# Power-of-two scales computed for pairs of attention units, all queue orders made anew, and more warming matmuls in the opening

## The chip, the cores and the metric

The kernel runs on one core of a Trainium2 chip. The time is device microseconds of one execution. PE is TensorE, DVE VectorE, ACT ScalarE, POOL GpSimd, SP the SyncE queue that issues all the kernel's transfers.

## What is computed

Attention with random features, then a feed-forward layer on all tokens. From the reference, cut:

```python
# q, k, v: 8 batches x 8 heads x 576 x 64; omega: 128 x 64
q_s, k_s = q / 64 ** .25, k / 64 ** .25
phi(x): h = x @ omega.T - sum(x * x) / 2;  exp(h - max(h)) / sqrt(128)
kv, z = phi(k_s).T @ v, sum over tokens of phi(k_s)
attn  = (phi(q_s) @ kv) / (phi(q_s) @ z + 1e-6)
x     = attn as 4608 tokens x 512
h     = x @ w_in                      # 512 x 2048
out   = max(0.01 * h, h) @ w_out      # 2048 x 512
```

## The kernel before

**Tiling.** The 4608 tokens are nine blocks of 512 (0 to 8). Heads go in pairs (`hp` 0 to 3). A *unit* is one pair of heads in one batch of keys or one block of queries: its features are 4 or 5 tiles of 128 tokens x 2 heads x 128 features. A key batch ends in the sums `kv` (L1262 in the opening, L1274 to L1276 later); a query block multiplies its features by them (L1388, L1381), divides (`r`, L1401 and L1403; `xp`, L1405) and turns the result into the input `xt` of the feed-forward layer (L1328 and L1331 in the opening, a DMA transpose L1316 later).

**The opening.** Key batches 0 and 1 and query block 0 are units of class `Whole`: inputs come transposed (L1106, tiles `nat`, `t`, `xn`, by their places in memory), PE multiplies in fp32 (L1133, 16 matmuls into the bank `pj`; the fifth tile of a key unit goes to `pj0` and `edge`), DVE takes the maximum (L1149) and subtracts it (L1151, into `ph`), ACT takes the exponent. At the same time the weights `w_in` and `w_out` are loaded in 1 MB pieces (L877), rebuilt from their halves of words (L892 to L922) and split into two fp16 parts (L758, L963).

**The omega constants.** `omega()` loads omega (L820) and the 128 x 128 identity (`ident`, L821). DVE scales omega and takes its largest magnitude (L832, L833), PE spreads that over all partitions by a product with `ident` (L799), DVE makes a power of two of it (L804 to L809) and `split` makes the fp16 `om` and the factor `om_c` (L838 to L843). The power and `split` are needed by units of class `Unit` only, thus not by the opening's fp32 units.

**The later units, class `Unit`.** There are 56: 24 key units (key batches 2 to 7, four pairs of heads each) and 32 query units (query blocks 1 to 8). `prepare()` loads `nat` (L1000), ACT squares it into `z` and adds the squares of each partition into column 0 of `sc` (L1003), DVE sums the squares of each head (`sq`, L1005) and makes four factors on 128 x 1 (L1010, L1012, L1014, L1015). They scale the halves of fp16 written into `z`, which a DMA transpose turns into `t` (L1028). PE then projects (L1041), and the features follow as above.

**The feed-forward layer.** Blocks 0 and 1 use plain products in the first layer (L1541), blocks 2 to 8 products with fewer multiplications whose weights come from memory through a ring (L1595); the second layer is L1777, in the last two blocks L1702. Sums go to the banks `ffn` and `late`.

**The order of the work.** It is written out: `ORDER` lists all operations by number, `ON` names the engine of those that have a choice, `PLACES` the buffer that each tile gets. Each engine executes its part of `ORDER` in that order, so an operation that waits holds all behind it on its engine. A negative number in `ORDER`, −n, is n warming matmuls on PE: a product of `ident` with itself (L850, 128 x 240) that nobody reads. They lie in a part of a bank that `mi` also has, so some wait for that bank.

Of the kernel before, what the change touches and what calls it, by code (L numbers as in the profile page):

```python
# [17 lines left out]
P = 128  # L18
# [63 lines left out]
    "raw": [0, 1, 3, 2, 0, 1, 3, 2, 3, 0, 1, 2],  # L82
    "sqz": [0, 1, 2, 0, 1, 2, 0, 1, 2, 0, 1, 2],
# [1800 lines left out]
```

## Time and profile before

| | |
|---|---|
| time, median of 3 runs (lowest to highest) | 902.92 us (900.46 to 908.13) |
| time of the profiled execution, and its span | 904.01 us, 902.2 us |
| mean granted clock of TensorE | 0.994 |
| PE, PEld (weight loads, which overlap PE) | 97%, 70% |
| DVE, ACT, POOL | 82%, 62%, 37% |

An engine's share is its busy time over the span. The granted clock is in parts of 2.4 GHz. A line such as L1149 is a line of the kernel before; where the kernel after is quoted, its own lines are used, with the old line beside them.

### The profile page before, as it was taken

What the parts mean: (1) busy time and instruction counts of PE and PEld (TensorE: products, weight loads), DVE (VectorE), ACT (ScalarE), POOL (GpSimd) and SP (SyncE); (2) the same over time, 40 slices, a digit from 0 to 9 for tenths busy, and PEclk for the clock granted to TensorE, in tenths of its full rate; (3) what the DMA queues carried; (4) which work ended last, traced back from release to release, by engine and by line L of the source; (5) the groups of instructions that cost most, each with busy time, mean ns of one, the idle gap of its engine ahead of it and who ended that gap; (6) DMA issues with size and microseconds to landing.
All of it is one profiled execution on the core that took longest, in us unless ns stands there. A gap on an engine that the chain in (4) does not pass through costs nothing.

```text
span 902.2 us, 20554 instructions
## 1 busy us (share of the span) xinstructions
PE 879.3 (97%) x8136; PEld 632.3 (70%) x8136; DVE 740.9 (82%) x1438; ACT 556.0 (62%) x997; POOL 330.6 (37%) x387
## 2 busy tenths in 40 slices
PE   6899999999999999999999999999999999999998
PEld 5786645555557865687558765876588656888887
DVE  6999999898988889878877998888878768884662
ACT  5789897678746775568647864763565633632430
POOL 1332557465343435225331622333222421331341
PEclk9999999999999999999999999999999999999999
...
GB/s 365 269 179 202 148 156 174 200 245 106 171 250 258 237 217 156 220 250 207 224 203 236 223 185 230 199 203 168 175 206 253 172 96 179 140 111 153 129 1 48
DMA packets 274881, 170.13 MB, mean 189 GB/s; under 512 B 191072, under 2 KB 237920, under 8 KB 273760
## 3 DMA queue, kind: packets, MB, share of 16 engines
...
q8 instruction: 63, 1.03, 0.5%
q14 instruction: 34, 0.28, 0.1%
HBM read 105.87 MB, written 16.78 MB: 136 GB/s over the span
## 4 chain that ended last, share of the span: by engine, by line
PE 80%; DVE 9%; DMA 5%; ACT 3%; issue 1%; SPq 1%; POOL 0%; DVEq 0%; ACTq 0%
PE ffn L1777 16%; PE late L1777 15%; PE ffn L1595 11%; PE late L1595 9%; PE ffn L1541 5%; PE pj L1041 5%; PE ffn L1702 5%; PE late L1541 4%; PE late L1702 3%; DMA out<-row 2%; DVE st L1149 1%; DVE ph L1151 1%; PE mi L1381 1%; PE mi L1262 1%; DMA qp<-ph 1%
## 5 line engine op out<-in xcount | busy, mean ns | idle before, releaser
L1595 PEld LDWEIGHTS <-w 128*128 128x128 f16 x2352 | 227.3, 98 | 36.0 <-issue 3.7
L1777 PEld LDWEIGHTS <-big 128*128 128x128 f16 x1344 | 128.0, 98 | 138.3
L758 POOL TENSOR_TENSOR big<-row,big 128x512 f16<-128x512 f32 x89 | 116.6, 1316 | 201.2 <-ACT big L752 128.7
L1777 PE MATMUL ffn<-wt,big 128*128 128x512 f16 x672 | 157.3, 379 | 0.0
L1777 PE MATMUL late<-wt,big 128*128 128x512 f16 x672 | 156.6, 379 | 0.0
L1595 PE MATMUL ffn<-xt,w 128*128 128x256 f16 x900 | 123.6, 273 | 0.6 <-DMA w<-w1d 0.6
L1595 PE MATMUL late<-xt,w 128*128 128x256 f16 x852 | 113.4, 273 | 1.5 <-ACT row L752 1.1
L1074 ACT ACTIVATE p<-pj,st,sc 128x128 f32<-128x128 f32 x224 | 81.0, 468 | 35.3 <-DVE st L1057 24.0
L1049 DVE TENSOR_REDUCE st<-pj 128x8 f32<-128x1024 f32 x68 | 73.2, 1077 | 13.6 <-PE pj L1041 13.4
L1063 POOL TENSOR_SCALAR st<-st,sc 128x8 f32<-128x8 f32 (+1 forms) x37 | 24.5, 663 | 145.0 <-DVE st L1049 125.4
L758 DVE TENSOR_TENSOR ph<-p,ph 128x1024 f16<-128x1024 f32 x56 | 70.2, 1254 | 6.4 <-ACT ph L752 6.3
L1080 ACT ACTIVATE p<-p,little 128x1024 f32<-128x1024 f32 (+1 forms) x40 | 38.1, 952 | 47.5 <-DVE p L1077 47.2
L752 ACT ACTIVATE big<-row 128x512 f16<-128x512 f32 x88 | 54.0, 624 | 19.6 <-DVE row L1567 19.2
L1541 PEld LDWEIGHTS <-w 128*128 128x128 f16 x384 | 36.5, 98 | 40.0
L1595 PE MATMUL ffn<-w,w 128*128 128x256 f16 x336 | 55.0, 273 | 0.2 <-ACT row L752 0.2
L1541 PE MATMUL ffn<-xt,w 128*128 128x512 f16 x216 | 51.7, 379 | 0.0
L752 ACT ACTIVATE ph<-p 128x1024 f16<-128x1024 f32 x47 | 49.6, 1056 | 1.2 <-PE mi L1276 0.7
L1003 ACT ACTIVATE z<-nat 128x512 f32<-128x512 f32 (+1 forms) x56 | 36.4, 650 | 22.6 <-DMA nat<-qn 10.0
L919 POOL TENSOR_TENSOR wt<-wt,wt 128x1024 f32<-128x1024 f32 x10 | 25.4, 2550 | 67.1 <-ACT wt L917 33.8
L1702 PEld LDWEIGHTS <-big 128*128 128x128 f16 x432 | 42.3, 98 | 4.9
L1077 DVE SCALAR_TENSOR_TENSOR p<-pj,sc,st 128x1024 f32<-128x1024 f32 (+1 forms) x40 | 41.6, 1039 | 4.6 <-POOL st L1067 3.9
L1595 PE MATMUL late<-w,w 128*128 128x256 f16 x264 | 43.2, 273 | 0.3 <-DVE row L748 0.3
...
## 6 DMA issues: line engine op xcount, KB each, us to landing
w<-w1d SPq DMA_DIRECT2D x196, 256.0 KB, 3.8
...
nat<-qn SPq DMA_DIRECT2D x32, 256.0 KB, 3.3
out<-row SPq DMA_DIRECT2D x30, 256.0 KB, 3.2
w1d<-wt SPq DMA_DIRECT2D x16, 256.0 KB, 3.6
...
```

Of the source, the lines that this page charges most:

```text
L752: ("ACT", act(n, int(pointer)), lambda: nc.scalar.activation(dst(), src(), AF.Copy, scale=1.0 if scale is None else value()), False),
L758: return ways([(e, c, lambda g=g: g.tensor_tensor(dst(), a(), b(), op=ALU.subtract), True) for e, c, g in (("POOL", pool_(n), nc.gpsimd), ...
L1003: op("ACT", act(n) + 0.16, lambda: nc.scalar.activation(square(), flat(at(nat)[:, :nt, :]), AF.Square, scale=SQ_SCALE, accum_out=at(self.s ...
L1041: nc.tensor.matmul(at(pj)[:, 512 * h + c * M:512 * h + (c + 1) * M], at(self.t)[:, 2 * (c0 + c) + h, :], om[:, w, :], start=(w == 0), stop ...
L1049: op("DVE", dve(n * M), lambda: nc.vector.tensor_reduce(row(0), pv(), axis=AX.X, op=ALU.max), r=[pj], w=[st], prio=prio)
L1074: nc.scalar.activation(p()[:, g], pv()[:, g], AF.Exp, bias=row(2)[:, g:g + 1], scale=down())
L1077: op("DVE", dve(n * M), lambda: nc.vector.scalar_tensor_tensor(p(), pv(), down(), row(2).rearrange("p (g o) -> p g o", o=1).broadcast_to([ ...
L1080: op("ACT", act(n * M, 1), lambda: nc.scalar.activation(flat(p()), flat(p()), AF.Exp, bias=shift), w=[p32], r=["ones"], prio=prio)
L1541: nc.tensor.matmul(at(ph), wk[wp][:, c:c + P], xt[:, 512 * xp:512 * xp + 512], start=(i == 0), stop=(i == 3 * KT - 1))
L1595: nc.tensor.matmul(pair(bank)[:, f], wt[:, k, wp, f * P:f * P + P], operand(xname, k, xp), start=(first and f == k == i == 0), stop=(k == ...
L1702: nc.tensor.matmul(pair(bank)[:, t], g()[:, gp, f, t * P:t * P + P], operand(wname, 2 * q + f, wp), start=(first and q == t == f == i == 0 ...
L1777: nc.tensor.matmul(at(po), g_(q)[:, s, gp, t * P:(t + 1) * P], wf[wp], start=(q == s == 0 and gp == wp), stop=(q == s == 3 and gp == 1))
```

## The change

**Scales for pairs.** The loop over head pairs now prepares two `Unit`s at once, at even `hp`. They share one `sc` tile of 8 columns (before: 4, one for each unit). The new `load()` of both runs first (transfer, squares, sums of squares), then the four scale operations once, on 128 x 2, then `parts()` of both. All else in a unit is the same, with its own column of `sc`.

```diff
-        "sc": (4, [P, 4], F32),
+        "sc": (4, [P, 8], F32),
...
-        def prepare(self):
+        def load(self, sc, x):
...
-               accum_out=at(self.sc)[:, 0:1]), r=[nat], w=[z, self.sc], prio=prio)
+               accum_out=at(sc)[:, x:x + 1]), r=[nat], w=[z, (sc, x)], prio=prio)
...
+        def prepare(self, other):
+            buf_sc = buf("sc")
+            for x, u in enumerate((self, other)):
+                u.load(buf_sc, x)
             def scales():
-                nc.vector.tensor_scalar(sc[:, 1:2].bitcast(U32), sc[:, 0:1].bitcast(U32), 1, 0x7F800000,
+                nc.vector.tensor_scalar(sc[:, 2:4].bitcast(U32), sc[:, 0:2].bitcast(U32), 1, 0x7F800000,
...
-                nc.vector.tensor_scalar(sc[:, 0:1], sc[:, 3:4], -1.0, None, op0=ALU.mult)
-            op("DVE", 0.5, scales, r=["om_c"], w=[self.sc], prio=prio)
+                nc.vector.tensor_scalar(sc[:, 0:2], sc[:, 6:8], -1.0, None, op0=ALU.mult)
+            op("DVE", 0.5, scales, r=["om_c"], w=[(buf_sc, 0), (buf_sc, 1)], prio=self.prio)
+            for u in (self, other):
+                u.parts()
...
-                u = Unit("k", b, hp, prio)
-                u.prepare()
+                if hp % 2 == 0:
+                    pair = Unit("k", b, hp, prio), Unit("k", b, hp + 1, prio)
+                    pair[0].prepare(pair[1])
+                u = pair[hp % 2]
...
-            u = Unit("q", j, hp, prio) if j else Whole("q", j, hp, prio)
-            if j:
-                u.prepare()
+            if j and hp % 2 == 0:
+                pair = Unit("q", j, hp, prio), Unit("q", j, hp + 1, prio)
+                pair[0].prepare(pair[1])
+            u = pair[hp % 2] if j else Whole("q", j, hp, prio)
```

**New tables.** `ORDER`, `ON` and `PLACES` are all new. In `ORDER` the warming matmuls were −9, −4, −4, −6, −5 (28 in all) and are −12, −25, −6, −4, −6, −10, −4, −4 (71). The first lines:

```diff
-    2, 0, 16, 183, 1, 62, 27, 3, 165, 43, 17, 151, 18, 184, 185, 4, 22, 28, 19, 81, 63, 23, 20, 144, 188, 7, 9, 5, -9,
+    2, 0, 16, 1, 144, 27, 151, 3, 183, 43, 17, 4, 22, 5, 6, 18, 23, 24, 28, 145, 33, 81, 146, 19, 62, 7, 152, 20, 9,
```

**DVE's first instructions.** After four fills of constants DVE's queue began so (omega's scaling and maximum, a step on a weight piece `wt`, the features of a unit, and then the power of two of omega, L804 to L809):

```order
L832 TENSOR_SCALAR xt_108<-xt_108 128x256
L833 TENSOR_REDUCE little<-xt_108 128x1
L900 TENSOR_SCALAR wt_74<-wt_73 128x1024
L1149 TENSOR_REDUCE st_112<-pj_129 128x8
L1149 TENSOR_REDUCE st_113<-pj_0_133 128x2
L1151 TENSOR_TENSOR ph_89<-pj_129,st_112 128x1024
L804 TENSOR_REDUCE little<-mi_136 128x1
L805 TENSOR_SCALAR little<-little 128x1
```

In the kernel after, the power (L803 to L808) and omega's split (L837 to L842, before L838 to L843) stand ahead of the first features (L1161 and L1163, before L1149 and L1151):

```order
L832 TENSOR_REDUCE little<-xt_108 128x1
L803 TENSOR_REDUCE little<-mi_136 128x1
L804 TENSOR_SCALAR little<-little 128x1
L806 TENSOR_SCALAR little<-little 128x1
L807 RECIPROCAL little<-little 128x1
L808 TENSOR_SCALAR little<-little 128x1
L837 TENSOR_SCALAR little<-little 128x1
L841 TENSOR_SCALAR om<-xt_108,little 64x128
L842 SCALAR_TENSOR_TENSOR om<-xt_108,little,om 64x128
L841 TENSOR_SCALAR om<-xt_108,little 64x128
L842 SCALAR_TENSOR_TENSOR om<-xt_108,little,om 64x128
L1161 TENSOR_REDUCE st_112<-pj_0_133 128x2
```

The power was behind the first unit's features, and the split some hundred instructions further back; both now come before any feature.

**SP's first transfers**, before (`xt` is omega's tile here):

```order
L820 DMA xt_108<-omT 128x256
L1106 DMA nat_83<-kT 128x640
L877 DMA big_81<-w_in 128x2048
L821 DMA ident<-eye 128x128
L1106 DMA t_87<-qT 128x512
L1106 DMA nat_84<-kT 128x640
```

and after:

```order
L819 DMA xt_108<-omT 128x256
L1118 DMA nat_83<-kT 128x640
L820 DMA ident<-eye 128x128
L876 DMA big_79<-w_in 128x2048
L1118 DMA t_87<-kT 128x640
L876 DMA big_82<-w_in 128x2048
```

The identity moved ahead of the first 1 MB piece of `w_in`, and the second unit loaded is one of keys, not of queries.

**PE just ahead of the first matmul of the feed-forward layer**, before (the last sums of key batch 1, then the first plain product):

```order
L1133 MATMUL pj_129<-xt_108,z_86 128x128 x2
L1262 MATMUL mi_137<-v_0_99,edge_92 128x65
L1262 MATMUL mi_137<-v_0_99,ph_91 128x65 x4
L1262 MATMUL mi_137<-v_0_99,edge_92 128x65
L1262 MATMUL mi_137<-v_0_99,ph_91 128x65 x4
L1541 LDWEIGHTS w_1_62
L1541 MATMUL late_841<-xt_109,w_1_62 128x512
```

and after (L849 is the warming matmul, L1342 the turn of `xp`, L1276 the sums, L1556 the plain product; before L850, L1328, L1262, L1541):

```order
L849 MATMUL mi_137<-ident 128x240
L1342 MATMUL ffn_135<-ident,xp_106 128x128 x4
L1276 MATMUL mi_136<-v_0_99,edge_92 128x65
L1276 MATMUL mi_136<-v_0_99,ph_89 128x65 x4
L1276 MATMUL mi_136<-v_0_99,edge_92 128x65
L1276 MATMUL mi_136<-v_0_99,ph_89 128x65 x4
L1276 MATMUL mi_136<-v_0_99,edge_93 128x65
L1276 MATMUL mi_136<-v_0_99,ph_91 128x65 x4
L1276 MATMUL mi_136<-v_0_99,edge_93 128x65
L1276 MATMUL mi_136<-v_0_99,ph_91 128x65 x4
L1556 LDWEIGHTS w_3_64
L1556 MATMUL late_907<-xt_109,w_3_64 128x512
```

Ten more sums, one more turn of `xp` and four of the last warming matmuls now stand there, ahead of the first product.

## Rows read from the trace of the kernel before

**Rows 1.** The page's busy time: engine, us (share of the span), instructions.
```profile
PE 879.3 (97%) x8136; PEld 632.3 (70%) x8136; DVE 740.9 (82%) x1438; ACT 556.0 (62%) x997; POOL 330.6 (37%) x387
```

**Rows 2.** Busy time by stretch (start:end us, length, then as named).
```profile
core 0: us, PE busy (x) PEld busy (x) DVE busy (x) ACT busy (x) POOL busy (x), PEclk, DMA share, GB/s
0.00:77.80 77.80, 63.89 (x737) 59.18 (x738) 67.61 (x115) 58.82 (x82) 23.52 (x19) 0.93 0.75 281
77.80:898.10 820.30, 815.36 (x7401) 573.12 (x7400) 672.45 (x1322) 497.20 (x917) 307.07 (x368) 1.00 0.76 180
...
16.00:22.00 6.00, 5.03 (x60) 5.04 (x62) 5.23 (x7) 2.72 (x3) 0.69 (x1) 0.72 1.03 416
33.00:38.00 5.00, 4.13 (x44) 3.91 (x44) 3.79 (x10) 4.56 (x8) 2.91 (x2) 0.66 0.99 395
```

**Rows 3.** The chain that ended last: start us, us, what.
```profile
127.85 2.59 PE late L1777 x12
```

**Rows 4.** PE's timeline: start us, us, what [idle before, releaser].
```profile
5.07 0.80 PE L1133 MATMUL pj<-xt,nat 64*128 64x128 f32 x4 [5.07 <-DMA nat<-kT]
...
10.42 1.10 PE L850 MATMUL mi<-ident 128*128 128x240 f16 x9
...
75.45 0.44 PE L1262 MATMUL mi<-v,edge 128*128 128x65 f32 x2 [0.96 <-DVE xp L1405]
...
77.78 2.76 PE L1541 MATMUL late<-xt,w 128*128 128x512 f16 x12
```

**Rows 5.** DVE's timeline in the opening.
```profile
8.70 0.69 DVE L900 TENSOR_SCALAR wt<-wt 128x1024 uint32<-128x1024 uint32 x1 [5.05 <-ACT wt L892]
...
12.01 0.28 DVE L804 TENSOR_REDUCE little<-mi 128x1 f32<-128x128 f32 x1
...
12.97 1.21 DVE L902 SCALAR_TENSOR_TENSOR wt<-big,wt 128x1024 uint32<-128x1024 uint32 x1
...
20.61 1.22 DVE L1149 TENSOR_REDUCE st<-pj 128x8 f32<-128x1024 f32 x1 [0.77 <-PE pj L1133]
...
28.28 1.48 DVE L1189 TENSOR_REDUCE little<-v 128x1 f32<-128x1280 f32 x1
29.68 1.21 DVE L1151 TENSOR_TENSOR ph<-pj,st 128x1024 f32<-128x1024 f32 x1
...
37.37 1.23 DVE L1149 TENSOR_REDUCE st<-pj 128x8 f32<-128x1024 f32 x1 [1.07 <-PE pj L1133]
...
70.01 0.42 DVE L1405 TENSOR_TENSOR xp<-mi,r 128x256 f32<-128x256 f32 x1
...
70.68 0.12 DVE L838 TENSOR_SCALAR little<-little 128x1 f32<-128x1 f32 x1
...
73.24 0.69 DVE L1331 TENSOR_TENSOR xt<-ffn,xt 128x512 f16<-128x512 f32 x1
```

**Rows 6.** SP's timeline: issues of transfers.
```profile
1.65 0.42 SPq L877 DMA_DIRECT2D big<-w_in  x1
2.11 0.43 SPq L821 DMA_DIRECT2D ident<-eye  x1
```

**Rows 7.** Transfers: count, KB each, median us from issue to landing.
```profile
nat<-qn SPq DMA_DIRECT2D x32, 256.0 KB, 3.3
...
xt<-v SPq DMA_TRANSPOSE x13, 4.6
...
ident<-eye SPq DMA_DIRECT2D x1, 64.0 KB, 5.6
```

**Rows 8.** DVE's timeline at the scales of one unit, first and next after.
```profile
80.08 0.15 DVE L1010 TENSOR_SCALAR sc<-sc 128x1 uint32<-128x1 uint32 x1
...
80.64 1.27 DVE L963 SCALAR_TENSOR_TENSOR w<-wt,little,w 128x1024 f16<-128x1024 f32 x1
```

**Rows 9.** PE's waits by line and releaser: us in all, times, longest.
```profile
PE mi L799 <- DVE xp L1405: 3.4, 2, 2.1
...
PE late L1595 <- DVE row L748: 0.3, 1, 0.3
PE late L1595 <- DVE row L1611: 0.3, 1, 0.3
```

**Rows 10.** SP's timeline at the input of block 2.
```profile
268.98 1.44 SPq L1316 DMA_TRANSPOSE xt<-v  x1
```

**Rows 11.** PE's timeline at the first product of block 2.
```profile
276.47 0.71 PE L1595 MATMUL ffn<-xt,w 128*128 128x256 f16 x5
```

More of the change, by code (lines that the diff above doesn't have):

```diff
@@ L78 @@
 PLACES = {
[1 row of a table removed]
[1 row of a table added]
     "v": [0, 0, 0, 0, 0, 0, 0],
     "kv": [0, 1, 0, 1, 0, 1, 0, 1, 0],
[L82 to L83 removed]
[2 rows of a table removed]
+    "raw": [0, 2, 1, 3, 0, 2, 3, 1, 2, 0, 1, 3],
+    "sqz": [0, 2, 1, 0, 2, 0, 1, 0, 1, 2, 0, 1],
[2 rows of a table added]
     "pj": [0, 0, 0, 0, 0, 0, 0, 0, 0, 0, 0, 0, 0, 0, 0, 0, 0, 0, 0, 0, 0, 0, 0, 0, 0, 0, 0, 0, 0, 0, 0, 0, 0, 0, 0, 0,
@@ L330 @@
-    1024: "DVE", 1046: "DVE", 1055: "DVE", 1058: "DVE", 1078: "DVE", 1081: "DVE", 1097: "DVE", 1108: "DVE",
-    1117: "DVE", 1125: "DVE", 1200: "POOL", 1210: "DVE", 1221: "DVE", 1227: "DVE", 1232: "POOL", 1235: "DVE",
-    1250: "DVE", 1255: "POOL", 1268: "POOL", 1295: "DVE", 1301: "POOL", 1306: "DVE", 1330: "POOL", 1335: "DVE",
-    1352: "POOL", 1357: "DVE", 1358: "DVE", 1366: "DVE", 1375: "DVE", 1387: "DVE", 1391: "DVE", 1398: "DVE",
-    1428: "DVE", 1432: "DVE", 1460: "DVE", 1477: "DVE", 1545: "DVE", 1572: "POOL", 1584: "DVE", 1590: "DVE",
@@ L345 @@
-    2409: "DVE", 2432: "DVE", 2437: "POOL", 2452: "DVE", 2454: "DVE", 2455: "DVE", 2463: "DVE", 2467: "DVE",
-    2476: "DVE", 2483: "DVE", 2484: "DVE", 2495: "DVE", 2507: "DVE", 2514: "DVE", 2519: "DVE", 2537: "DVE",
-    2545: "DVE", 2546: "DVE", 2550: "DVE", 2560: "DVE", 2568: "DVE", 2579: "DVE", 2580: "DVE", 2635: "DVE",
-    2647: "POOL", 2657: "DVE", 2664: "DVE", 2673: "DVE", 2681: "DVE", 2696: "DVE", 2714: "POOL", 2718: "DVE",
-    2719: "DVE", 2730: "POOL", 2745: "POOL", 2750: "DVE", 2756: "DVE", 2761: "POOL", 2774: "POOL", 2784: "POOL",
@@ L350 @@
-    2796: "POOL", 2802: "DVE", 2812: "DVE", 2818: "DVE", 2846: "DVE", 2850: "DVE", 2866: "DVE", 2874: "DVE",
-    2878: "DVE", 2883: "DVE", 2901: "DVE", 2906: "DVE", 2912: "DVE", 2915: "DVE", 2936: "DVE", 2939: "DVE",
-    2942: "DVE", 2988: "DVE", 2997: "DVE", 3009: "DVE", 3015: "DVE", 3030: "DVE", 3046: "DVE", 3082: "POOL",
-    3085: "DVE", 3095: "POOL", 3118: "POOL", 3122: "DVE", 3123: "DVE", 3129: "DVE", 3134: "POOL", 3172: "DVE",
-    3175: "DVE", 3187: "DVE", 3195: "DVE", 3204: "DVE", 3210: "DVE", 3215: "DVE", 3221: "DVE", 3233: "DVE",
@@ L355 @@
-    3236: "DVE", 3245: "DVE", 3248: "DVE", 3262: "DVE", 3277: "DVE", 3292: "DVE", 3297: "DVE", 3330: "DVE",
-    3355: "DVE", 3366: "DVE",
+    104: "DVE", 339: "DVE", 344: "DVE", 349: "DVE", 359: "DVE", 360: "DVE", 365: "DVE", 385: "DVE", 440: "DVE",
+    456: "DVE", 477: "POOL", 491: "DVE", 508: "DVE", 541: "DVE", 545: "POOL", 558: "DVE", 581: "DVE", 593: "DVE",
+    617: "DVE", 629: "DVE", 641: "DVE", 664: "DVE", 665: "DVE", 671: "DVE", 696: "DVE", 702: "DVE", 711: "DVE",
+    712: "DVE", 717: "DVE", 721: "DVE", 732: "DVE", 737: "DVE", 741: "DVE", 817: "DVE", 843: "POOL", 868: "POOL",
@@ new lines @@
+    881: "POOL", 897: "POOL", 899: "DVE", 948: "DVE", 980: "POOL", 996: "POOL", 997: "DVE", 1000: "DVE", 1013: "DVE",
+    1029: "DVE", 1034: "DVE", 1044: "DVE", 1052: "DVE", 1060: "DVE", 1066: "DVE", 1071: "DVE", 1084: "DVE",
+    1091: "DVE", 1096: "DVE", 1102: "DVE", 1115: "DVE", 1120: "DVE", 1125: "DVE", 1146: "DVE", 1196: "DVE",
+    1209: "POOL", 1214: "DVE", 1244: "POOL", 1275: "DVE", 1284: "POOL", 1292: "POOL", 1294: "DVE", 1297: "DVE",
+    1309: "DVE", 1327: "POOL", 1342: "POOL", 1343: "POOL", 1348: "DVE", 1356: "DVE", 1365: "DVE", 1369: "DVE",
@@ new lines @@
+    1381: "DVE", 1387: "DVE", 1399: "DVE", 1412: "DVE", 1418: "DVE", 1430: "DVE", 1449: "DVE", 1458: "DVE",
+    1467: "DVE", 1493: "DVE", 1503: "DVE", 1538: "DVE", 1553: "POOL", 1561: "POOL", 1567: "POOL", 1590: "POOL",
+    1603: "POOL", 1608: "DVE", 1619: "POOL", 1620: "DVE", 1621: "DVE", 1641: "POOL", 1648: "POOL", 1651: "DVE",
+    1658: "DVE", 1668: "DVE", 1685: "POOL", 1698: "POOL", 1713: "POOL", 1715: "DVE", 1731: "DVE", 1740: "DVE",
+    1747: "DVE", 1752: "DVE", 1753: "DVE", 1759: "DVE", 1762: "DVE", 1771: "DVE", 1778: "DVE", 1779: "DVE",
@@ new lines @@
+    1784: "DVE", 1790: "DVE", 1810: "DVE", 1820: "DVE", 1824: "DVE", 1884: "DVE", 1909: "DVE", 1912: "DVE",
+    1925: "POOL", 1927: "DVE", 1942: "DVE", 1947: "POOL", 1960: "POOL", 1976: "POOL", 1977: "DVE", 1990: "DVE",
+    1998: "POOL", 2001: "DVE", 2006: "POOL", 2008: "DVE", 2011: "DVE", 2020: "DVE", 2028: "POOL", 2031: "DVE",
+    2044: "POOL", 2056: "POOL", 2059: "DVE", 2070: "DVE", 2079: "DVE", 2082: "DVE", 2083: "DVE", 2101: "DVE",
+    2105: "DVE", 2133: "DVE", 2141: "DVE", 2153: "DVE", 2163: "DVE", 2164: "DVE", 2172: "DVE", 2175: "DVE",
@@ new lines @@
+    2186: "DVE", 2207: "DVE", 2217: "DVE", 2260: "POOL", 2270: "DVE", 2284: "DVE", 2304: "POOL", 2317: "POOL",
+    2320: "POOL", 2333: "POOL", 2334: "DVE", 2362: "POOL", 2372: "DVE", 2399: "POOL", 2417: "DVE", 2427: "POOL",
+    2428: "POOL", 2429: "DVE", 2433: "DVE", 2441: "DVE", 2442: "DVE", 2445: "DVE", 2466: "DVE", 2467: "DVE",
+    2473: "DVE", 2484: "DVE", 2492: "DVE", 2497: "DVE", 2498: "DVE", 2503: "DVE", 2504: "DVE", 2512: "DVE",
+    2515: "DVE", 2534: "DVE", 2538: "DVE", 2543: "DVE", 2546: "DVE", 2547: "DVE", 2552: "DVE", 2558: "DVE",
@@ new lines @@
+    2568: "DVE", 2626: "DVE", 2631: "POOL", 2653: "DVE", 2656: "DVE", 2664: "DVE", 2677: "POOL", 2679: "DVE",
+    2689: "POOL", 2691: "DVE", 2694: "DVE", 2712: "POOL", 2722: "DVE", 2737: "DVE", 2742: "POOL", 2745: "DVE",
+    2770: "POOL", 2771: "POOL", 2773: "DVE", 2775: "DVE", 2776: "DVE", 2786: "DVE", 2804: "DVE", 2818: "DVE",
+    2820: "DVE", 2822: "DVE", 2836: "DVE", 2840: "DVE", 2860: "DVE", 2875: "DVE", 2880: "DVE", 2886: "DVE",
+    2889: "DVE", 2910: "DVE", 2921: "DVE", 2942: "DVE", 2957: "DVE", 2983: "DVE", 2995: "DVE", 3031: "DVE",
@@ L357 @@
+    3062: "POOL", 3080: "DVE", 3091: "POOL", 3092: "DVE", 3093: "DVE", 3095: "DVE", 3096: "DVE", 3113: "POOL",
+    3116: "DVE", 3126: "POOL", 3141: "POOL", 3144: "DVE", 3147: "DVE", 3159: "DVE", 3176: "DVE", 3179: "DVE",
+    3193: "DVE", 3200: "DVE", 3205: "DVE", 3217: "DVE", 3223: "DVE", 3237: "DVE", 3246: "DVE", 3258: "DVE",
+    3261: "DVE", 3275: "DVE", 3287: "DVE", 3299: "DVE", 3302: "DVE", 3308: "DVE",
 }
@@ L997, in prepare @@
             nat, z, t = buf("nat"), buf("z"), buf("t")
-            self.t, self.sq, self.sc = t, buf("sq"), buf("sc")
+            self.nat, self.z, self.t, self.sq, self.sc, self.x = nat, z, t, buf("sq"), sc, x
             src = (kn if self.what == "k" else qn)[self.hp, self.t0:self.t0 + n, :]
@@ L1017, in prepare, with parts @@
+            op("DVE", 0.5, scales, r=["om_c"], w=[(buf_sc, 0), (buf_sc, 1)], prio=self.prio)
+            for u in (self, other):
+                u.parts()
+        def parts(self):
+            nt, prio, nat, z, t, sc, x = self.nt, self.prio, self.nat, self.z, self.t, self.sc, self.x
+            n = nt * P
             heads = lambda: at(nat)[:, :nt, :].rearrange("p c (h d) -> p (c h) d", d=D)
-            up = lambda: at(self.sc)[:, 2:3]
+            up = lambda: at(sc)[:, 4 + x:5 + x]
             zh, zl = lambda: at(z)[:, :2 * nt, :D], lambda: at(z)[:, :2 * nt, D:]
@@ L1020, in prepare @@
             if self.i < Z_POOL[self.what]:
-                high(n, heads, heads, up, r=[self.sc], w=[nat], prio=prio)
+                high(n, heads, heads, up, r=[(sc, x)], w=[nat], prio=prio)
                 high(n, zh, heads, psum=True, r=[nat], w=[z], prio=prio)
@@ L1024, in prepare @@
             else:
-                high(n, zh, heads, up, psum=True, r=[nat, self.sc], w=[z], prio=prio)
+                high(n, zh, heads, up, psum=True, r=[nat, (sc, x)], w=[z], prio=prio)
                 op("DVE", stt(n) + 0.07, lambda: nc.vector.scalar_tensor_tensor(zl(), heads(), up(), zh(),
-                   op0=ALU.mult, op1=ALU.subtract), port=True, r=[nat, self.sc], w=[z], prio=prio)
+                   op0=ALU.mult, op1=ALU.subtract), port=True, r=[nat, (sc, x)], w=[z], prio=prio)
             op("SP", 1.55, lambda: nc.sync.dma_start(out=at(t)[:, :2 * nt, :], in_=flat(at(z)[:, :2 * nt, :]),
@@ L1044, in features @@
             op("PE", 4 * nc_ * 0.056, project, r=[self.t, "om"], w=[pj], prio=prio, slack=SLACK["t"])
-            down = lambda: at(self.sc)[:, 3:4]
+            down = lambda: at(self.sc)[:, 6 + self.x:7 + self.x]
             sq = lambda: at(self.sq)[:, g0:g0 + n].rearrange("p (c h) -> p h c", h=2)
@@ L1055, in bias @@
                 if straight:
-                    nc.vector.scalar_tensor_tensor(rows(1), rows(0), at(self.sc)[:, 0:1], sq(), op0=ALU.mult, op1=ALU.add)
+                    nc.vector.scalar_tensor_tensor(rows(1), rows(0), at(self.sc)[:, self.x:self.x + 1], sq(), op0=ALU.mult, op1=ALU.add)
                     nc.vector.scalar_tensor_tensor(rows(2), rows(1), EXP_SHIFT, sq(), op0=ALU.add, op1=ALU.subtract)
@@ L1062, in bias_apart @@
             def bias_apart():
-                nc.gpsimd.tensor_scalar(row(1), row(0), at(self.sc)[:, 0:1], None, op0=ALU.mult)
+                nc.gpsimd.tensor_scalar(row(1), row(0), at(self.sc)[:, self.x:self.x + 1], None, op0=ALU.mult)
                 nc.gpsimd.tensor_tensor(rows(1), rows(1), sq(), op=ALU.add)
@@ L1074, in exps @@
                         nc.scalar.activation(p()[:, g], pv()[:, g], AF.Exp, bias=row(2)[:, g:g + 1], scale=down())
-                op("ACT", n * 0.37, exps, r=[pj, st, self.sc, "ones"], w=[p32], prio=prio)
+                op("ACT", n * 0.37, exps, r=[pj, st, (self.sc, self.x), "ones"], w=[p32], prio=prio)
             else:
```

35 lines of the change are left out of this document (10 added, 25 removed), and 418 rows, old and new, of tables (ORDER, PLACES).

## The prediction

> **What bounds the kernel now.** I read the busy times by stretch first [rows 2]. They split at 77.8 us, where PE begins its first product of the feed-forward layer [rows 4]. From there to 898.1 us PE is busy for 815.4 of 820.3 us at a granted clock of 1.00: it idles for 4.9 us in all. Is it at its pace while busy? The chain that ended last shows 12 products of 512 columns in 2.59 us [rows 3], 0.216 us each, or 512 columns in 518 cycles of 2.4 GHz. So behind 77.8 us every microsecond is PE's own work, and what other engines gain there is worth at most what they take away of 4.9 us. Behind 898.1 lie 4.1 us to the span's end, in which the last tile is finished and stored. Ahead of 77.8 PE is busy for 63.9 us only, at clocks that fall to 0.72 and 0.66 in two of its stretches; there DVE has 67.6 us of work, and 5.05 of its 10.2 idle us lie ahead of its first step on data, at 8.70 [rows 2, 5]. PE's last wait before the first product ends on DVE's `xp` [rows 4]. The opening is thus bound by DVE's list of work, the rest by PE.
>
> The sum is made against the profiled execution: 904.0 us with a span of 902.2, that is 1.1 us above the median of the three runs. The rule for the parts: a microsecond counts if it lies on DVE's list ahead of the first product, or on PE behind it.
>
> **Part 1, omega's constants go to the front: −3.5 us.** The five steps of the power took DVE from 12.01 to 12.97, 0.96 us, and the split from 70.68 to 73.24, 2.56 us [rows 5]. Together 3.52 us leave the stretch in which DVE is the bound, and go into the 5.05 us in which it stood idle. That holds if `ident` has landed early, since the power waits for a PE product with it. `ident` was issued at 2.11 us behind a 1 MB piece of `w_in` and took 5.6 us, landing at 7.7 [rows 6, 7]. Now it is issued in the slot of that piece, at 1.65, ahead of it. `nat`, issued in the slot before and ahead of the piece, had landed at 5.07, when PE began [rows 4]. If `ident` lands there too, 3.52 us of DVE's work end near 8.7, where its first step on data stood: full gain. If it still takes 5.6 us it lands at 7.25, the work ends near 10.8, 2.1 us past 8.70, and 1.4 us are gained. I take the first: `ident` is 64 KB with no large transfer ahead of it. Bounds −3.5 and −1.4.
>
> **Part 2, other work ahead of the first product: +0.5 us.** By the two orders DVE does 105 instructions from its first step on data to the `xp` that the last wait of PE ends on, and 108 in the kernel after. Besides part 1 there is one subtraction into `ph` more, 1.21 us, one `xp` with its two `r` steps more, 0.67 us (from 70.01 to 70.68), and one maximum over `v` (L1189) less, 1.40 us from its start to that of the next [rows 5]. That is 1.21 + 0.67 − 1.40 = 0.48. The ten sums and the turn of `xp` that PE now does ahead of the first product were done behind it before; PE has the same list in all, so they move the first product and not the end. Bounds 0 (the extra `ph` and `xp` only come early) and +0.5; I take +0.5, since DVE is the bound there.
>
> **Part 3, 43 more warming matmuls: −0.9 us.** They cost PE time: nine took 1.10 us at 10.42 [rows 4], 0.12 us each, so 43 are 5.3 us. PE idles for 13.9 us in the opening [rows 2] and 53 of the 71 stand early, in PE's waits for DVE; the waits are their cover. The last three groups (−10, −4, −4: 18) stand close to the first product, some behind waits for the bank of `mi`. Without cover they cost 18 x 0.12 = 2.2 us. I take nothing: the last wait there ends on DVE, whose work is not changed by them. What they may bring is clock. In 16 to 22 us the granted clock was 0.72, in 33 to 38 us it was 0.66, PE being busy for 5.0 of 6 and 4.1 of 5 us [rows 2]; in just these stretches DVE waited for PE's fp32 products, 0.77 and 1.07 us [rows 5]. At full clock both waits could go: between 0 and −1.8 us. I take half, −0.9. Bounds −1.8 and +2.2.
>
> The clock of those stretches lies between its two levels, 1.2 and 2.4 GHz: PE spent a part of them at the lower one. The Trainium skill, "TensorE: Matmul & The Clock Gate", section "What's actually happening", says that the slow state is the default and activity releases it; the rows agree so far as PE waited in both stretches, but no run yet shows that activity of this kind raises it. By that rule alone the whole 1.8 us would come back, and the sum would be lower by 0.9.
>
> **Part 4, shared scales: −0.5 us.** One unit's four scale steps took DVE from 80.08 to 80.64, 0.56 us [rows 8]. 56 units make 224 such steps; pairs make 112 on two columns. No row has a step of two columns; from below it costs what the one-column step does, from above twice, which would save nothing. I take the first: in part 2 an `xp` on 128x256 and two steps on 128x4 take 0.67 us together, so width costs little here. So DVE does 28 x 0.56 = 15.7 us less. But all of that lies behind 77.8 us or is spread over the last units before it, and there PE is the bound. Of its 4.9 idle us, 3.4 − 2.1 = 1.3 us end on an `xp` (the other wait of that line is the opening's) and twice 0.3 us on `row` [rows 9], 1.9 in all that end on DVE. With DVE's list 2% shorter I take a quarter of these, 0.5. Bounds: −4.9, if new orders remove all the idle time, and +2, if a new order brings as much again as DVE's share of it.
>
> **The sum:** −3.5 + 0.5 − 0.9 − 0.5 = −4.4, so 904.0 − 4.4 = **899.6 us**. By the bounds of parts 1 to 3 alone it lies between −5.3 and +1.3, by rows.
>
> **Rivals.**
> *A smoother plan.* As above, but the new order also removes nearly all idle time behind 77.8: −3.9 − 4.9 gives 895. For it: only 4.9 us in some thirteen waits have to go. Against it: they end on ACT, DVE and transfers alike, and any new order makes its own.
> *DVE bounds the kernel.* Then the 15.7 us come off the time: 904.0 − 15.7 = 888.3. For it: PE's weight loads and matmuls overlap and its 97% may be filled by waiting in them, with DVE next at 82% [rows 1]. Against it: 0.216 us for each product of 512 columns is PE's own pace [rows 3], and a PE held by DVE would show it as waits. [...]
> *The change brings nothing.* `ident` lands as late as before (−1.4), the clock stays down (0), other work costs +0.5 and the last warming matmuls lie bare (+2.2 at most, half of it 1.1): 0.2 more, 904. For it: the 16 DMA engines are busy for 0.75 of the opening [rows 2], so a transfer issued early need not land early.
> *Slower: pairs hold their loads.* The scales of the first unit of a pair now wait for the second's `nat` and its squares. If the second load starts only when the first is done, the features of a pair come a load of 3.3 us later [rows 7]. Block 2 is the first that needs both a key batch and a query block of `Unit`s, two pairs each: four pairs, 13.2 us. What lies spare there: its input is turned by a transfer issued at 268.98 that lands 4.6 us later, at 273.6, and PE's first product of the block is at 276.47 [rows 7, 10, 11], 2.9 us. So 13.2 − 2.9 = 10.3 us would show, and with the −4.0 of the others 904.0 + 10.3 − 4.0 = 910.3. It decides from 1.7 us for each pair (4 x 1.7 = 2.9 + 4.0). Against it: `nat` has two buffers, so the second load runs beside the first, and DVE comes to block 2 with some 30 instructions less.
>
> **How the numbers follow.** The forecast, with its own range of 897 to 902 us, gets 0.43; the smoother plan 0.18; DVE as the bound 0.08; nothing 0.20; slower 0.11. The likeliest gives 899.6. The range leaves out DVE as the bound below (0.08) and the worse part of the slower case above (0.07), so it goes from 891 to 908 us. A measurement here tells a change of about 1%, 9 us, from none: below 893.9 and above 911.9. Faster by that is DVE as the bound and a smoother plan with its luck (0.06 of its 0.18): 0.14. Slower is the larger half of the last rival: 0.06. Within 1% stays 0.80.
>
> **What the profile after would show.** Part 1: DVE does L803 to L842 before 9 us, and has no such steps near 70 us. Part 2 and 3: the first L1556 product near 77.8 − 3.9 = 73.9 us plus the ten sums that PE now does ahead of it (two took 0.44 us at 75.45 [rows 4], so ten 2.2), near 76 us, and a clock over 0.72 and 0.66 in PE's early stretches. Part 4: DVE's busy time at about 725 us, PE's unchanged but for the 5.3 us of warming. Behind the first product PE idle for 3 to 6 us. Wrong would be: PE's idle time there over 10 us with releasers in `sc`, `z` or `t` (the slower rival), or a span shorter than PE's list (DVE as the bound).

## The result and the profile after

| | before | after |
|---|---|---|
| median of 20 runs (lowest to highest) | 901.95 us (898.51 to 908.13) | 909.9 us (906.1 to 912.5) |
| profiled execution, and its span | 904.01 us, 902.2 us | 909.21 us, 907.3 us |

After takes 1.0086 of before's time (95% interval 1.0069 to 1.0103), 8 us more. I had forecast 4 us less. The range ended at 908.0, and the time lies above it. One of the six executions of the run e4_no_warming below took 2778 us and is left out of its ratio.

The page of the kernel after, busy time by engine, answers to [rows 1]. DVE has 98 instructions less and is as busy as before; 725 us were forecast.

```profile
PE 883.1 (97%) x8179; PEld 632.6 (70%) x8179; DVE 741.7 (82%) x1340; ACT 549.4 (61%) x987; POOL 318.9 (35%) x373
```

Its busy time by stretch, columns as in [rows 2], cut at PE's first product of the feed-forward layer and among its last ones (here, and in e2_shape below, 0.2 to 0.3 us ahead of the end of the last product):

```profile
0.00:75.90 75.90, 66.72 (x803) 61.44 (x804) 68.63 (x121) 61.82 (x86) 23.50 (x19) 1.00 0.76 278
75.90:903.00 827.10, 816.14 (x7378) 571.13 (x7377) 672.21 (x1218) 487.57 (x902) 295.44 (x354) 1.00 0.76 180
```

In this one profile the opening came out as forecast: first product at 75.90 us, where I had "near 76", and a granted clock of 1.00, 0.93 before. The loss is behind it. Before took 820.3 us for that stretch; the ten sums and the turn that moved ahead of it are 2.65 us (2.2 at 0.22 each and 0.43 for the turn), so after should take 817.65. It takes 827.1, 9.5 us more. PE idles for 11.0 us in it and not 4.9, and is busy for 3.4 us more than it should be. Its two longest waits there, of a kind that took 0.3 us in all before ([rows 9], L1595 behind L1611), are these (L1626 was L1611):

```profile
PE ffn L1610 <- DVE row L1626: 2.3, 1, 2.3
PE late L1792 <- DVE row L1626: 1.5, 1, 1.5
```

PE's timeline of the kernel after shows the first product, and the longest of the waits behind it with the work that follows it:

```profile
75.90 2.75 PE L1556 MATMUL late<-xt,w 128*128 128x512 f16 x12
...
517.75 0.49 PE L1610 MATMUL ffn<-xt,w 128*128 128x256 f16 x3 [2.28 <-DVE row L1626]
518.07 0.80 PE L1610 MATMUL ffn<-w,w 128*128 128x256 f16 x3
```

What kept DVE from that `row`? DVE's timeline just ahead of it, and POOL's beside it:

```profile
513.08 1.63 DVE L1015 TENSOR_SCALAR sc<-sc 128x2 uint32<-128x2 uint32 x1
514.75 1.08 DVE L1017 TENSOR_SCALAR sc<-sc 128x2 uint32<-128x2 uint32 x1
515.74 0.31 DVE L1019 TENSOR_SCALAR sc<-sc,little 128x2 f32<-128x2 f32 x1
516.08 1.02 DVE L1020 TENSOR_SCALAR sc<-sc 128x2 f32<-128x2 f32 x1
517.02 0.68 DVE L1626 TENSOR_TENSOR row<-ffn,row 128x512 f32<-128x512 f32 x1
```

```profile
512.55 2.14 POOL L757 TENSOR_TENSOR xn<-xp,xn 128x1024 f16<-128x1024 f32 x1 [3.17 <-ACT xn L751]
514.64 1.16 POOL L757 TENSOR_TENSOR big<-row,big 128x512 f16<-128x512 f32 x1
515.75 0.28 POOL L1221 CAST v<-v 128x20 f16<-128x20 f32 x1
515.92 1.15 POOL L757 TENSOR_TENSOR big<-row,big 128x512 f16<-128x512 f32 x1
```

The four shared scale steps take 4.0 us here, where one unit's took 0.56 [rows 8]. Each ends when POOL's instruction ends: 513.08 + 1.63 = 514.71 and 512.55 + 2.14 = 514.69; 515.83 and 515.80; 516.05 and 516.03; 517.10 and 517.07. So these steps on two columns wait for POOL. PE then waits 2.28 us, and from 517.7 to 521.6 us it runs at a granted clock of 0.56, most of that time at the lower of its two levels (1.2 GHz). By an estimate from that clock this costs 3.9 x 0.44 = 1.7 us more:

```profile
517.70:521.60 3.90, 3.85 (x34) 2.69 (x34) 2.19 (x8) 3.63 (x5) 1.15 (x1) 0.56 0.00 0
```

Is that place one of many? The instructions of the first of the four lines, in the kernel before and in the kernel after (shortest/median/longest in ns):

```profile
L1010 DVE TENSOR_SCALAR sc<-sc x56: 123/145/155, 80.1 to 684.3; 128x1 uint32<-128x1 uint32 x56
```

```profile
L1015 DVE TENSOR_SCALAR sc<-sc x28: 152/209/1632, 76.7 to 686.2; 128x2 uint32<-128x2 uint32 x28
```

Before, none of the 224 steps was over 0.21 us; after, the longest of each line is above 1 us. All four lines together: 36.8 us for 224 steps before, 34.0 us for 112 after. The steps were halved, and their time fell by 2.8 us instead of 15.7 (in start-to-start time; 18.4 in busy time).

The same over the whole trace, instruction by instruction: 26 of after's 112 steps last more than 0.25 us, and each of these 26 ends 0.02 to 0.03 us after an instruction of POOL. In the kernel before 109 of the 224 steps run wholly within one instruction of POOL, and none of them is held. Not every instruction of POOL holds a step on two columns: four short ones of after run within a TENSOR_SCALAR of POOL.

### The profile page after: what moved, and what is told of

Its sections match the earlier page's. It is cut to its first block, busy times and chain, and to the rows that moved or that the text cites. A ratio compares the mean times of both kernels' runs of the same rounds, so it can differ in the third digit from the quotient of the medians.

```text
span 907.3 us, 20508 instructions
## 1 busy us (share of the span) xinstructions
PE 883.1 (97%) x8179; PEld 632.6 (70%) x8179; DVE 741.7 (82%) x1340; ACT 549.4 (61%) x987; POOL 318.9 (35%) x373
## 4 chain that ended last, share of the span: by engine, by line
PE 70%; DVE 15%; DMA 5%; ACT 4%; issue 2%; SPq 2%; POOL 1%; DVEq 0%; ACTq 0%
PE ffn L1610 13%; PE late L1792 12%; PE ffn L1792 11%; PE late L1610 10%; PE late L1717 6%; PE pj L1053 4%; PE ffn L1556 4%; PE late L1556 3%; PE ffn L1717 2%; DVE ph L757 2%; DMA nat<-qn 1%; DVE p L1089 1%; PE mi L1276 1%; DMA t<-z 1%; DVE sq L1003 1%
## 5 line engine op out<-in xcount | busy, mean ns | idle before, releaser
L1792 PEld LDWEIGHTS <-big 128*128 128x128 f16 x1344 | 128.2, 98 | 138.5 <-issue 1.8
L757 POOL TENSOR_TENSOR big<-row,big 128x512 f16<-128x512 f32 x83 | 104.8, 1272 | 185.2 <-ACT big L751 118.0
L1610 PE MATMUL late<-xt,w 128*128 128x256 f16 x792 | 108.0, 273 | 1.9 <-ACT row L1633 1.3
L757 DVE TENSOR_TENSOR ph<-p,ph 128x1024 f16<-128x1024 f32 x56 | 72.9, 1301 | 10.9 <-ACT ph L751 10.5
L1556 PEld LDWEIGHTS <-w 128*128 128x128 f16 x384 | 36.8, 98 | 41.2 <-issue 0.2
L1075 POOL TENSOR_SCALAR st<-st,sc 128x8 f32<-128x8 f32 (+1 forms) x31 | 15.2, 490 | 140.6 <-DVE st L1061 115.6
L1610 PE MATMUL ffn<-w,w 128*128 128x256 f16 x372 | 61.5, 275 | 0.6 <-DVE row L747 0.4
L751 ACT ACTIVATE big<-row 128x512 f16<-128x512 f32 x76 | 46.9, 628 | 6.7 <-DVE row L1582 6.4
L1556 PE MATMUL ffn<-xt,w 128*128 128x512 f16 x216 | 50.3, 379 | 0.0
L762 POOL TENSOR_TENSOR xp<-xp 128x256 f32<-128x256 f32 (+1 forms) x25 | 27.3, 1090 | 54.4 <-DVE xp L762 27.8
L1003 DVE TENSOR_REDUCE sq<-z 128x8 f32<-128x512 f32 (+1 forms) x56 | 39.1, 703 | 5.3 <-ACT z L1001 5.2
L751 ACT ACTIVATE ph<-p 128x1024 f16<-128x1024 f32 x41 | 43.3, 1056 | 0.3
```

Source lines behind the costliest of these rows:

```text
L751: ("ACT", act(n, int(pointer)), lambda: nc.scalar.activation(dst(), src(), AF.Copy, scale=1.0 if scale is None else value()), False),
L757: return ways([(e, c, lambda g=g: g.tensor_tensor(dst(), a(), b(), op=ALU.subtract), True) for e, c, g in (("POOL", pool_(n), nc.gpsimd), ...
L1003: op("DVE", dve(n), lambda: nc.vector.tensor_reduce(at(self.sq)[:, :2 * nt], square().rearrange("p (g d) -> p g d", d=D), axis=AX.X, op=AL ...
L1556: nc.tensor.matmul(at(ph), wk[wp][:, c:c + P], xt[:, 512 * xp:512 * xp + 512], start=(i == 0), stop=(i == 3 * KT - 1))
L1610: nc.tensor.matmul(pair(bank)[:, f], wt[:, k, wp, f * P:f * P + P], operand(xname, k, xp), start=(first and f == k == i == 0), stop=(k == ...
L1792: nc.tensor.matmul(at(po), g_(q)[:, s, gp, t * P:(t + 1) * P], wf[wp], start=(q == s == 0 and gp == wp), stop=(q == s == 3 and gp == 1))
```

## The experiments

Two theories. **Lock**: a scale step on more than one column cannot run beside POOL's instructions, ends late on DVE, and PE waits. **Order**: the new tables are slower by themselves. A third question is what the opening's parts are worth. Ratios are to runs of the kernel before on the same chip; 0.001 is 0.9 us.

| run | base and edit | ratio (95%) | longest scale step |
|---|---|---|---|
| e1_apart | after, steps on 128x1 | 1.0005 (0.9983 to 1.0026) | 0.21 us |
| e2_shape | after, steps 3x2 into 2x3 | 0.9991 (0.9972 to 1.0009) | 0.21 us |
| e10_strided | after, columns four apart | 1.0115 (1.0089 to 1.0141) | 1.64 us |
| e3_before_wide | before, steps on 128x2 | 1.0290 (1.0255 to 1.0325) | 2.06 us |
| e11_odd | before, steps on 128x3 | 1.0291 (1.0269 to 1.0314) | 2.06 us |
| e4_no_warming | after, no warming | 1.0099 (1.0068 to 1.0130) | |
| e6_shape_no_warming | e2_shape, no warming | 1.0019 (1.0003 to 1.0035) | 0.21 us |
| e8_more_warming | before, 56 warming matmuls | 1.0002 (0.9989 to 1.0015) | |
| e5_omega_early | before, omega first | 1.0020 (1.0001 to 1.0039) | |
| e7_omega_features_first | e5, weight piece later | 1.0008 (0.9988 to 1.0027) | |
| e9_both | e7 and e8 | 0.9992 (0.9978 to 1.0007) | |

**e1_apart.** The pairs, the order and the places stay; a pair's four steps are done column by column.

```diff
-                nc.vector.tensor_scalar(sc[:, 2:4].bitcast(U32), sc[:, 0:2].bitcast(U32), 1, 0x7F800000,
+                for x in range(2):
+                    nc.vector.tensor_scalar(sc[:, 2 + x:3 + x].bitcast(U32), sc[:, x:x + 1].bitcast(U32), 1, 0x7F800000,
...
```

> The changed kernel with its own order, but the four scale steps of a pair done column by column: eight steps on 128x1 where it has four on 128x2. In the changed kernel 112 steps on 128x2 take 34.0 us, single ones up to 1.6 us and ending with the instruction that POOL runs beside them; in the kernel before 224 steps on 128x1 take 36.8 us, none over 0.21. Lock theory (a step of two columns has to wait for POOL, one of one column does not): no scale step above 0.25 us, 224 of them about 36.6 us; PE's waits of 2.3, 1.5 and 0.8 us behind them (517, 608, 210 us) and the 1.7 us lost at a granted clock of 0.56 behind the first go, some 6 us: 903 to 905 us. Order theory (the new order is slower whatever the steps do): 908 to 911 us.

901.4 us, less than the 903 to 905 of the lock theory: with twice as many steps some 7 us came back, by the ratios. The 224 steps take 36.3 us one by one (28.6 where overlaps count once), none over 0.21. The first line's steps, and the stretch behind the first product:

```profile
L1016 DVE TENSOR_SCALAR sc<-sc x56: 136/144/154, 79.6 to 679.7; 128x1 uint32<-128x1 uint32 x56
```

```profile
78.78:896.40 817.62, 813.26 (x7378) 570.37 (x7377) 665.82 (x1330) 487.60 (x902) 295.70 (x354) 1.00 0.76 182
```

After's order takes 817.6 us there once the steps have one column. The order theory falls.

**e2_shape.** As many steps as after, each on a repeated pair, with other sizes for input and output.

```diff
+                three = lambda i: sc[:, 6 * i:6 * i + 2].rearrange("p (o x) -> p o x", o=1).broadcast_to([P, 3, 2])
+                six = lambda i: sc[:, 6 * i:6 * i + 6].rearrange("p (a b) -> p a b", a=2)
-                nc.vector.tensor_scalar(sc[:, 2:4].bitcast(U32), sc[:, 0:2].bitcast(U32), 1, 0x7F800000,
+                nc.vector.tensor_scalar(six(1).bitcast(U32), three(0).bitcast(U32), 1, 0x7F800000,
...
```

> The changed kernel, its four shared scale steps kept (112 in all), but each reads its two columns as 3 x 2 (the pair repeated three times) and writes 2 x 3 columns, of which the first two are used. The Trainium skill, VectorE: DVE Perf Modes, section What auto-detection actually checks, has the fast mode with both ports only where the outermost sizes of input and output are both even or equal; here they are not. Apart from that page: lock theory with this form outside of it: no step above 0.3 us, 112 steps 19 to 23 us in all, DVE's busy time 12 us lower than in the changed kernel, 902 to 905 us. If the form of the operands does not matter: steps up to 1.6 us as in the changed kernel, 908 to 911 us. Order theory: 908 to 911 us whatever the steps take.

899.59 us, less than the 902 to 905 of the lock theory. The first line's steps, and the stretch behind the first product (at 75.08 us):

```profile
L1017 DVE TENSOR_SCALAR sc<-sc x28: 142/148/159, 75.9 to 675.9; 128x6 uint32<-128x6 uint32 x28
```

```profile
75.08:892.60 817.52, 812.82 (x7377) 570.26 (x7377) 659.69 (x1218) 487.68 (x902) 296.67 (x354) 1.00 0.77 182
```

Six elements are faster than two, and the steps take 19.0 us in all; 54 of the 112 run wholly within one instruction of POOL, and none is held. The stretch takes 817.5 us, what the kernel before takes for the same work (817.65), with 4.7 us of PE idle. So 9.6 of after's 827.1 us come with the form of the steps. The rest of the change shows no effect behind the first product, by the profiles of e1_apart and e2_shape.

**e3_before_wide.** The kernel before, nothing shared, but with a second column in each step.

```diff
-                nc.vector.tensor_scalar(sc[:, 1:2].bitcast(U32), sc[:, 0:1].bitcast(U32), 1, 0x7F800000,
+                nc.vector.tensor_scalar(sc[:, 2:4].bitcast(U32), sc[:, 0:1].bitcast(U32).broadcast_to([P, 2]), 1, 0x7F800000,
...
```

> The kernel before, order and units as they were, but each of a unit's four scale steps works on two columns (both from the same sum), 224 steps on 128x2; nothing is shared. Lock theory: the steps are stretched where POOL works beside them, as in the changed kernel (14 us over for 112), thus some 28 us over for 224, single ones above 1 us; PE waits behind some of them, 905 to 912 us. Order theory: 901 to 903 us.

927.52 us, more than the 905 to 912 that I expected: the 224 steps take 79.2 us, 42 over the 36.8 of before, and I had expected 28 over. Of the 224, 50 last more than 0.25 us, and each of these ends 0.02 to 0.03 us after an instruction of POOL. Behind the first product PE idles for 21.5 us, where it idled for 4.9 before:

```profile
77.50:922.90 845.40, 823.86 (x7402) 574.25 (x7400) 710.37 (x1322) 497.16 (x917) 301.35 (x368) 1.00 0.73 175
```

The lock appears in the old order too: with twice the steps it costs 26 us by the ratio, where after loses 9 against e2_shape.

**e10_strided, e11_odd.** Which form brings the lock? In e10_strided the pair's columns lie four apart (the first two lines below); in e11_odd a unit's steps have three columns (the last line).

```diff
+                sc = at(buf_sc).rearrange("p (x k) -> p x k", x=2)
+                nc.vector.tensor_scalar(sc[:, :, 1].bitcast(U32), sc[:, :, 0].bitcast(U32), 1, 0x7F800000,
...
+                nc.vector.tensor_scalar(sc[:, 3:6].bitcast(U32), sc[:, 0:1].bitcast(U32).broadcast_to([P, 3]), 1, 0x7F800000,
...
```

> The changed kernel, its four shared scale steps on 128x2 with the two columns four apart in memory instead of side by side. The lock by what the steps did so far: steps on 128x1 and on 3 x 2 into 2 x 3 were never stretched, steps on 128x2 were. If it is the count of two in both operands that matters: steps up to 1.6 us as in the changed kernel, 908 to 911 us. If it is that the columns are side by side: no step above 0.3 us, 899 to 901 us as in e2_shape.

> The kernel before, order and units as they were, each of a unit's four scale steps on three columns (all from the same sum), 224 steps on 128x3; with two columns the time was 927.5 us. If any width above one, the same for input and output, is stretched: steps above 1 us, 920 to 930 us. If only even widths are: no step above 0.3 us, 900 to 902 us.

909.72 and 925.82 us, both in the range of the lock theory. The second line of e10_strided and of e11_odd:

```profile
L1017 DVE TENSOR_SCALAR sc<-sc x28: 169/170/1081, 76.1 to 684.1; 128x2 uint32<-128x2 uint32 x28
```

```profile
L1012 DVE TENSOR_SCALAR sc<-sc x56: 169/170/2057, 77.6 to 710.6; 128x3 uint32<-128x3 uint32 x56
```

Neither the distance of the columns nor an odd count helps. The forms that waited have more than one column and the same outer size in and out; those that did not have one column, or different outer sizes.

The Trainium skill, "VectorE: DVE Perf Modes", section "What auto-detection actually checks", has the mode with two ports where a single source and the destination lie in SBUF and their outermost sizes, those of one left aside, are both even or equal. The Trainium skill, "SBUF — State Buffer", section "Who interferes with whom", says that between DVE in such a mode and GpSimd the one that issues first has the shared ports for its whole instruction, and the other is blocked. Four of the five forms agree with the two rules: 1.0 to 2.1 us for the longest of a line in the three forms that they put into the mode, 0.21 for e2_shape, which they keep out. A step on one column has no outermost size but one, so the rule as cited does not decide it; here none took over 0.21. The runs show the wait and which forms have it; that ports are the reason stands on these pages alone.

**e4_no_warming, e6_shape_no_warming, e8_more_warming.** The negative numbers of `ORDER` are taken out, or raised to −12, −25, −8, −6, −5 in the kernel before.

> The changed kernel without any of its 71 warming matmuls, all else as it is. If they hold the clock up as the forecast had it: the granted clock of the opening falls from 1.00 to about 0.93 or below, the first product of the feed-forward layer comes 1 to 2 us later than 75.9, and the time is 1 to 2 us longer, 911 to 912. If they only cost PE time: the first product comes up to 2 us earlier, 908.

> The changed kernel with its shared scale steps reading 3 x 2 and writing 2 x 3 columns (as in the run e2_shape, 899.6 us), and none of its warming matmuls. If the warming is worth what the forecast took (0.9 us, at most 1.8): 900.5 to 901.5 us. If it only costs PE time: 899 us or less.

> The kernel before with its five groups of warming matmuls at -12, -25, -8, -6, -5 (56) instead of -9, -4, -4, -6, -5 (28), nothing else changed. The two profiles of the kernel before differ by 3.9 us at the first product (77.8 and 73.9), with granted clocks in 16 to 22 and 33 to 38 us of 0.72 and 0.66 in the one, 1.00 in the other. If warming holds the clock: 1.00 there, the first product near 74, the median 1 to 2.5 us lower, 898.5 to 900, and a smaller spread. If it does nothing but cost PE time: 901 to 903.

910.8, 902.25 and 900.88 us. Without warming the granted clock of the opening is 0.95 (e4_no_warming) and 0.91 (e6_shape_no_warming) and not 1.00, as expected. The first product came at 75.32 us in the one, not later than after's 75.90, and at 78.51 in the other, later than e2_shape's 75.08. Taking the warming away raises the ratio by 0.0013 (from after) and 0.0028 (from e2_shape), and adding some to the kernel before leaves it where it was, with a clock of 1.00 and the first product at 74.84 us in its profile. Only the 0.0028 is clear of its noise, and barely: 0.0004 to 0.0052, an estimate from the two intervals. A worth of 0 to 2.5 us fits; the term of 0.9 is neither confirmed nor refuted.

**before_again.** One more profile of the kernel before.

> The kernel before once more, for a second profile of it: how much of its 77.8 us opening and of its 4.9 us of PE's idle time behind it belongs to the one execution that was profiled. If the execution was typical: first product of the feed-forward layer at 77.5 to 78, 4.5 to 5.5 us idle behind it. If it was slow by its opening: first product 1 to 3 us earlier, span near 899.

The first product came at 73.90 us and the span was 898.9. The two cold stretches of [rows 2] were not there:

```profile
16.00:22.00 6.00, 4.11 (x64) 3.73 (x64) 6.00 (x9) 3.77 (x5) 0.05 (x1) 1.00 1.03 415
33.00:38.00 5.00, 5.00 (x71) 4.64 (x67) 4.83 (x14) 4.55 (x8) 4.42 (x2) 1.00 0.99 395
```

So the execution from which I worked lost 3.9 us in its opening, with a clock that another execution of the same kernel does not show.

The other traces show how wide this goes. Four profiles have the opening of the kernel before (the two of it, e3_before_wide and e11_odd, whose edits act behind it), with the first product at 77.8, 73.9, 77.5 and 75.1 us. Four have after's opening (after, e1_apart, e2_shape, e10_strided), with 75.9, 78.8, 75.1 and 75.1 us, each at a clock of 1.00. One profile of each cannot tell the two openings apart, and after's "near 76" was in part luck.

**e5_omega_early, e7_omega_features_first, e9_both.** Numbers 1, 4, 5 and 6 of `ORDER` (the identity's transfer, PE's product, the power, the split) moved as in the change, in the kernel before; then 184 and 185 (the first steps on the piece of `w_in`) moved behind the first features; then also the warming of e8_more_warming.

```diff
-    2, 0, 16, 183, 1, 62, 27, 3, 165, 43, 17, 151, 18, 184, 185, 4, 22, 28, 19, 81, 63, 23, 20, 144, 188, 7, 9, 5, -9,
+    2, 0, 16, 1, 183, 62, 27, 3, 4, 5, 6, 165, 43, 17, 151, 18, 184, 185, 22, 28, 19, 81, 63, 23, 20, 144, 188, 7, 9, -9,
```

> The kernel before with its own order, but omega's power and split moved to DVE's first steps and the identity's transfer ahead of the first piece of w_in, as in the changed kernel; no other part of the change. Opening term of the forecast: the last wait of PE ahead of the first product of the feed-forward layer ends 3.5 us earlier, that product comes at about 74.3 instead of 77.8, and as PE is the bound behind it, the time falls by 3 to 4 us, 897 against 900.6. If the opening's clock and transfers decide where it ends and not DVE's list: within 1 us of the kernel before.

> As e5_omega_early (the kernel before with omega's power and split first and the identity ahead of w_in), but ACT's and DVE's first steps on the piece of w_in (L892, L900) stand behind the first unit's features, which do not need it. In e5_omega_early DVE stood still for 3.55 us until that piece, which had landed 2.4 us later than in the kernel before. If that wait ate the gain of the early constants: DVE goes on with features near 9.5 us, PE's wait of 4.6 us at 14.5 us is gone, and the time is 2 to 4 us below e5_omega_early's 1.002 of the kernel before: 897 to 900. If the opening ends where its transfers let it, whatever DVE's list: 901 to 903 as e5_omega_early.

> e7_omega_features_first and e8_more_warming together. If both help: 895 to 898 us, below both kernels. If the opening is set by its transfers: 900 to 903.

903.09, 901.56 and 899.96 us. e5_omega_early is slower, if barely clear of 1, not 3.5 us faster. DVE's timeline of e5_omega_early, the end of the split and the next step:

```profile
7.24 0.35 DVE L843 SCALAR_TENSOR_TENSOR om<-xt,little,om 64x128 f16<-64x128 f32 x1
11.14 0.69 DVE L900 TENSOR_SCALAR wt<-wt 128x1024 uint32<-128x1024 uint32 x1 [3.55 <-ACT wt L892]
```

The split was done at 7.6 us, and DVE then stood still: ACT could start on the piece of `w_in` at 9.99 us only (7.54 before, and 7.00 to 8.19 in five profiles with the old order of transfers), as the piece landed 2.4 us later behind the 64 KB of the identity. The features were queued behind it. That this stall is what costs the 1.8 us is not shown: the first product of this profile came at 77.21 us, within the spread above, and the stretch behind it took 823.1 us, 2.7 more than before. With the features first (e7_omega_features_first) the ratio is back at 1, and not below. With warming too it is 0.9992 (between my two ranges, as e8_more_warming was), the best of these, and that cannot be told from 1 either: no version here is shown to beat the kernel before.

## Why the prediction was wrong, point by point

- **What bounds the kernel: right, and it decided more than I took from it.** Behind the first product the time is PE's list plus PE's waits. That holds for after too; DVE as the bound (888.3 us) fell: in e2_shape DVE has 12.6 us less to do than after (729.1 us), and the stretch is no shorter than that of the kernel before. (The 4.9 us that PE waits there in the kernel before are nine waits, not the "some thirteen" that I gave the smoother plan.)
- **Part 4, the price of a shared step: the step that failed.** I wrote that no row has a step of two columns, took the price of one column, and put twice that above it; I chose the lower end because "width costs little here". The rows that I leaned on were an `xp` and an `r` step that read PE's banks, and a reciprocal, another operation. The 112 steps took 34.0 us, 0.30 each: in the sum within my two bounds (half of 36.8, and 36.8) but close to the upper one, and single steps took eleven times the price of one column. What I left out is the wait for POOL. It falls on few steps, and PE waits behind those, so a mean price hides it. The bound of +2 us on what DVE can cost PE was wrong with it: it was 9.6.
- **The row that was there.** The split of omega has two equal instructions, and in the trace of before they differ by five times. DVE's and POOL's timelines of the kernel before:

```profile
70.72 1.42 DVE L842 TENSOR_SCALAR om<-xt,little 64x128 f16<-64x128 f32 x1
...
72.53 0.29 DVE L842 TENSOR_SCALAR om<-xt,little 64x128 f16<-64x128 f32 x1
```

```profile
69.70 2.36 POOL L919 TENSOR_TENSOR wt<-wt,wt 128x1024 f32<-128x1024 f32 x1
```

  The first ends at 72.14, 0.08 us after POOL's long instruction (72.06); the second has only copies of some 0.2 us of POOL beside it. In before_again the two take 1.43 and 0.29 us. I had both in the 2.56 us of part 1 and did not ask why they differ. That was the price of a wide step beside POOL, and it would have made a rival. In the kernel after the same split takes 1.46 us at the front.
- **Part 1: its steps came as told, its gain did not.** In the kernel after the split ended at 7.75 us, the identity having landed near 5:

```profile
5.01 0.26 PE L798 MATMUL mi<-ident,little 128*128 128x128 bf16 x1 [5.01 <-DMA ident<-eye]
```

  But alone (e5_omega_early) the move costs 1.8 us (0.1 to 3.5) where I had −3.5. What I left out is who is late next: the piece of `w_in` that lost its slot, and the queue behind it, on which DVE stood still for 3.55 us. How much of the missing gain is due to that stays open.
- **Part 2** can't be told apart from it. The 2.2 us for ten sums hold, though I misread their row: its "x2" are two records of one sum. After's 20 sums run from 71.49 to 75.90 us, 0.22 each. **Part 3**: the clock was 1.00 as hoped for, but the kernel before has that in its second profile with 28 warming matmuls, so the profile of after does not show that the 43 did it.
- **The sum's base.** I knew that the profiled execution was 1.1 us above the median of three runs. Against 901.95, the median of 20 runs, it was 2.1 above, and its opening was 3.9 us longer than that of the second profile; part of what parts 1 and 3 were to win back was not lost in a usual execution. Without the lock the change is worth −0.8 us (e2_shape, −2.5 to +0.8), not −4.4.
- **The slower rival had the sign and not the cause.** Its time, 910.3 us (910.4 with the −3.9 of parts 1 to 3, where I wrote −4.0), came close, and PE's idle time behind the first product passed the 10 us that I had named as its mark. But that mark asked for releasers in `sc`, `z` or `t`, and the longer waits of after end on `row` and `p`. Pairs that hold their loads should show in e1_apart and e2_shape too, which keep the pairs; they cost nothing there. The right direction here was luck.
- **Where the 8 us went:** +9.6 behind the first product by the lock (6.3 us more of PE's waits than in e2_shape, some 1.7 at the lower clock behind one of them, 1.6 that I can't place), and about −0.8 by the rest: 8.8 in all, where 7.8 was measured (6.2 to 9.3). The share of the clock belongs to this execution: e10_strided has no such place behind its first product, and PE's waits there are 6.7 us longer than in e2_shape.
